# Later due times for some loads in a list scheduler, and two heads' running sums copied by engines instead of DMAs

## The chip, the core and the metric

The kernel runs on one core of a Trainium2 chip. The metric is the device time of one execution in microseconds (us). A core has five engines with queues of their own: TensorE (PE, with its weight loads shown apart as PEld), VectorE (DVE), ScalarE (ACT), GpSimd (POOL) and SyncE (SP), which here only issues DMAs. ACT can issue DMAs too. Work on different engines is ordered by semaphores alone.

## The reference

The kernel computes causal attention with a learned decay, and a two-layer network on its output:

```python
B, H, S, D = 8, 8, 576, 64
scores = q @ k.T / sqrt(D)
cum = np.cumsum(np.log(np.clip(f, 1e-4, 1.0)), axis=-1)
scores = where(causal, -1e9, scores + cum[:, :, :, None] - cum[:, :, None, :])
attn = softmax(scores); x = (attn @ v) as (B*S, H*D)
h = x @ w_in                              # 4608 x 512 @ 512 x 2048
out = (max(h, 0) + alpha * min(h, 0)) @ w_out
```

## The kernel before

The 64 heads are taken in 32 pairs `n` (four pairs to a batch). For a pair, PE makes the scores (line 332, tiles `k`, `q` or `KA`, `KB`, `QA`, `QB`), DVE takes the row maximum (L676, L594), ACT the exponentials (L552), PE transposes them (L565) and multiplies by `v`. The sums of the exponentials are inverted, written to DRAM (`rd`) and read back broadcast into the tile `ri` (L651); DVE multiplies the unnormalised output `xs` by `ri` (L744), and ACT and POOL split the product into a high and a low part (L746, L748), the `x` of the first layer. The first layer (`ffn1`) runs batch by batch, PE writing PSUM banks that ACT (L819) and DVE (L821) empty into `hs`; the second layer follows when attention is done.

The order on every engine is written by a list scheduler (`Plan`) while the program is built. Each operation has an engine, a duration in ns reckoned by a formula, a key and dependencies; the scheduler keeps a clock for each engine and repeatedly takes the operation that can start earliest (of equals, the lowest key). What it puts into an engine's queue is executed in that order on the chip, however long the waits then are. A DMA is reckoned by the issue, a shared channel of 220 KB/us and 1.0 us. An operation on the engine `"-"` issues nothing: it only takes time in the scheduler, in one queue that all of them share. The products of the first layer have the highest keys, so they fill whatever time attention leaves on PE.

The first eight pairs (`n < NN`) multiply in fp32, with two extra rows in the tiles `q` and `k` that add the decay: `cum` and plus or minus 8. For later pairs the tiles are split in two fp32r parts; their raw loads `rq` and `rk` (L488, L489) are rounded by DVE (L433), and POOL takes the remainders (L499, L504).

At the start, SP loads `f` (L345), `q` and `k` of the first pair (L443, L444). DVE clips `f` (L351), ACT takes the logarithm (L354), DVE scans (L357) in two parts, columns 0 to 255 and 256 to 575. SP and ACT then copy the sums of heads 0 and 1 by nine small DMAs (L454, L457) into the rows of `q` and `k`, as DMAs can write to any partition. POOL sets the constant rows (L373 to L375), the mask, the identity and a selection matrix. Meanwhile PE runs 21 matrix products on ones (L395) that nothing reads. SP goes on with the loads of pair 1, writes the sums of the first heads to DRAM (L362 to L364) and fetches the rows of later pairs from there (L461 to L463).

Of the kernel before, what the change touches and what calls it, by code (L numbers as in the profile page):

```python
# [8 lines left out]
F32 = mybir.dt.float32  # L9
# [9 lines left out]
NP = H // 2  # L19
# [164 lines left out]
def attention_moe(  # L184
# [79 lines left out]

    ctx_0 = ExitStack()
    p0 = ctx_0.enter_context(tc.tile_pool(name="p0", bufs=1))
    rqk = Ring(Store([(p0.tile([66, QW], F32, name=f"q0_{i}"), p0.tile([66, 2 * S], F32, name=f"k0_{i}")) for i in range(2)]))
    bch = Buf(Ring(Store([hs.rearrange("p a n -> p (a n)")[0 : B * H, 0 : 2 * S].bitcast(F32R).rearrange("p (t s) -> p t s", t=2)])))
    wbf = p0.tile([128, 512], BF16, name="wbf")
    sel = p0.tile([9, 6, 128], F32, name="sel")  # L270
# [62 lines left out]


    bft, bz, bcu = Buf(re), Buf(re), Buf(re)
    fl = lambda b: b.t[0 : B * H]
    ft, z, cu = (lambda: fl(bft)), (lambda: fl(bz)), (lambda: fl(bcu))
    chl = lambda: bch.t
    c32 = lambda: chl().bitcast(F32)
    cqf = cq.rearrange("k b t s -> (k b) t s")  # L340
# [1 line left out]

    o_w1 = op("POOL", 100, lambda: po.memset(warm, 1.0), -102)
    o_w2 = op("ACT", 1400, lambda: ac.activation(warm, warm, AF.Ln), -102, [o_w1])
    o_f = op("SP", 500, lambda: sy.dma_start(ft(), f.rearrange("b h s -> (b h) s")), -100, (), [bft], kb=144)  # L345
    o_z = op("DVE", 500, lambda: ve.memset(z(), 0.0), -100, (), [bz])

    o_clip, o_ln, o_sc = [], [], []
    PC = ((0, 256), (256, S))
    for a0, a1 in PC:  # L350
        o_clip.append(op("DVE", 130 + (a1 - a0), lambda a0=a0, a1=a1: ve.tensor_scalar(  # L351
            ft()[:, a0:a1], ft()[:, a0:a1], 1e-4, 1.0, ALU.max, ALU.min), -100, [o_f], [bft]))
    for i, (a0, a1) in enumerate(PC):
        o_ln.append(op("ACT", c_act(a1 - a0) + 180, lambda a0=a0, a1=a1: ac.activation(ft()[:, a0:a1], ft()[:, a0:a1], AF.Ln), -100, [o_clip[i]], [bft]))  # L354
    o_warm = op("ACT", 1500, lambda: ac.activation(warm, ft()[0:1, 0:1], AF.Exp), -99, o_ln, [bft])
    for i, (a0, a1) in enumerate(PC):
        o_sc.append(op("DVE", 100 + 2.2 * (a1 - a0), lambda i=i, a0=a0, a1=a1: ve.tensor_tensor_scan(  # L357
            cu()[:, a0:a1], ft()[:, a0:a1], z()[:, a0:a1], cu()[:, a0 - 1 : a0] if i else 0.0, ALU.add, ALU.add),
            -100, [o_ln[i], o_z] + o_sc, [bft, bz, bcu]))
    o_scan = o_sc[1]  # L360

# [7 lines left out]
        eng.memset(QB[64:68, S:640].bitcast(F32), 0.0)  # L369

    def eights(eng, i):
        q, k = rqk.store.items[i]
        eng.memset(q[64:66], -8.0)  # L373
        eng.memset(k[64:66], 8.0)
        eng.memset(q[64:66, S:640], 0.0)  # L375

    o_8 = [op("POOL", 2500, lambda i=i: eights(po, i), -101 + 5 * i) for i in range(2)]
    o_id = op("POOL", 600, lambda: make_identity(nc, ident), -98)

    def make_mask():  # L380

# [9 lines left out]

    o_wbf = op("DVE", 300, lambda: ve.memset(wbf, 1.0), -102)  # L392
    bw = Buf(rP)
    for i in range(7):
        op("PE", 800, lambda: [pe.matmul(bw.t, wbf[:, 0:128], wbf, start=True, stop=True) for _ in range(3)], -200, [o_wbf], [bw])  # L395

    def select():
# [7 lines left out]
            po.affine_select(sel[:, 4 + h, 64 * h : 64 * h + 64], sel[:, 4 + h, 64 * h : 64 * h + 64], pattern=[[0, 64]], base=-4,  # L405
                             channel_multiplier=1, compare_op=ALU.not_equal, fill=1.0)

    o_sel = op("POOL", 4000, select, 0.3, [o_mask])

    def zeros():  # L410
        for t in rT4.store.items:
            po.memset(t[64:128], 0.0)

    o_eps = op("POOL", 100, lambda: po.memset(eps, 1e-9), -97)
    o_zero = op("POOL", 400, zeros, -96)
    o_al = op("SP", 400, lambda: sy.dma_start(al, alpha), -4, [o_scan], kb=8)

    def signs():
# [17 lines left out]
    def early(n):  # L436
        return s_0[8 * (NN - 2)] if n == NN else None

    def load_0(n, bqk):

        b, p = divmod(n, NP)
        key = -60 if n == 0 else NS * n - 16
        ld = [op("SP", 450, lambda: sy.dma_start(bqk.t[0][0:64], qq[b, p, 0:64]), -99 if n == 0 else -59 if n == 1 else key, [o_scan] if n else (), [bqk], kb=304),  # L443
              op("SP", 450, lambda: sy.dma_start(bqk.t[1][0:64], kk[b, p, 0:64]), -99 if n == 0 else -59 if n == 1 else key, [o_scan] if n else (), [bqk], kb=288)]  # L444
        n_r = len(plan.ops)
        qr, kr = (lambda: bqk.t[0][65:66]), (lambda: bqk.t[1][64:65])
        halves = lambda ap: ap.rearrange("p (h s) -> p h s", h=2)
        rows = [[[], []] for _ in range(2)]
        if n == 0:

            for part, (a0, a1) in enumerate(PC):
                todo = [(a0, 0, a0, a1), (704 + a0, 1, a0, min(a1, S - 64))] + [(640, 1, S - 64, S)] * part
                for o, i, j0, j1 in todo:
                    rows[i][part].append(op("SP", 350, lambda o=o, i=i, j0=j0, j1=j1: sy.dma_start(  # L454
                        qr()[:, o : o + j1 - j0], cu()[i : i + 1, j0:j1]), key, [o_sc[part], o_8[n % 2]], [bcu, bqk], kb=2))
                for i in range(2):
                    rows[i][part].append(op("ACT", 600, lambda i=i, a0=a0, a1=a1: ac.dma_start(kr()[:, S * i + a0 : S * i + a1], cu()[i : i + 1, a0:a1]),  # L457
                                            -99.5, [o_sc[part], o_8[n % 2]], [bcu, bqk]))
        else:
            oo = [o_d0, o_d1, o_d2, o_8[n % 2]]  # L460
            k_ = op("SP", 350, lambda: sy.dma_start(halves(kr()), c0[0, 2 * n : 2 * n + 2].rearrange("(o h) s -> o h s", o=1)), key, oo, [bqk], kb=5)  # L461
            rows[0][0] += [k_, op("SP", 350, lambda: sy.dma_start(qr()[:, 0:S], c0[0, 2 * n : 2 * n + 1]), key, oo, [bqk], kb=2)]
            rows[1][0] += [k_, op("SP", 350, lambda: sy.dma_start(qr()[:, 640:QW], c0[1, 2 * n + 1 : 2 * n + 2]), key, oo, [bqk], kb=2)]  # L463
        c_rows.append(plan.ops[n_r:])
        return [(ld + r[0], ld + r[0] + r[1]) for r in rows]
# [17 lines left out]
    def load_n(n, bQ, bX):  # L483

        b, p = divmod(n, NP)
        kl, kc, bh = NS * n - 16, NS * n - 7, b * H + 2 * p
        bq, bk = Buf(rrq), Buf(rrk)
        l_q = op("SP", 450, lambda: sy.dma_start(bq.t, qq[b, p]), kl, [o_cl, early(n)], [bq], kb=608)  # L488
        l_k = op("SP", 450, lambda: sy.dma_start(bk.t, kk[b, p]), kl, [o_cl, early(n)], [bk], kb=576)  # L489
        QA, QB, KA, KB = ((lambda j=j: bQ.t[j]) for j in range(4))  # L490
        qc, kc_, rdy = [], [], []
        for a0, a1 in pieces(QW, 2):
            qc.append(round_(n, a1 - a0, lambda a0=a0, a1=a1: (QA()[:, a0:a1], bq.t[:, a0:a1]), kc, [l_q], [bq, bQ]))
        for a0, a1 in pieces(2 * S, 2):
            kc_.append(round_(n, a1 - a0, lambda a0=a0, a1=a1: (KA()[:, a0:a1], bk.t[:, a0:a1]), kc, [l_k], [bk, bQ]))
        qb = op("SP", 400, lambda: sy.dma_start(QB()[0:64, 0:QW].bitcast(F32), QA()[0:64].bitcast(F32)), kc, qc, [bQ], kb=304)
        rdy.append(qb)
        for i, (a0, a1) in enumerate(pieces(QW, 4)):
            rdy.append(op("POOL", c_po(a1 - a0), lambda a0=a0, a1=a1: po.tensor_tensor(  # L499
                QA()[64:128, a0:a1], bq.t[64:128, a0:a1], QA()[64:128, a0:a1].bitcast(F32), ALU.subtract),  # L500
                kc, [qc[i // 2], qb], [bq, bQ]))
        n_l = len(rdy)
        for i, (a0, a1) in enumerate(pieces(2 * S, 4)):
            rdy.append(op("POOL", c_po(a1 - a0), lambda a0=a0, a1=a1: po.tensor_tensor(  # L504
                KB()[0:64, a0:a1], bk.t[0:64, a0:a1], KA()[0:64, a0:a1].bitcast(F32), ALU.subtract),
                kc, [kc_[i // 2]], [bk, bQ]))
        rdy_x = load_x(n, bQ, bX, qc, rdy[n_l:])
        q2 = lambda: QB()[66:68].rearrange("p (h s) -> p h s", h=2)[:, :, 0:S].bitcast(F32)
        k2 = lambda: KB()[64:66].rearrange("p (h s) -> p h s", h=2).bitcast(F32)
        oo = [o_c0, o_c1, o_c2] + o_one  # L510
        rdy.append(op("SP", 350, lambda: sy.dma_start(k2(), cq[0, bh : bh + 2].rearrange("h t s -> t h s")), kc, oo, [bQ], kb=9))
        rdy.append(op("SP", 350, lambda: sy.dma_start(q2(), cqf[bh : bh + B * H + 2 : B * H + 1].rearrange("h t s -> t h s")),
                      kc, oo, [bQ], kb=9))
        return rdy, rdy_x
# [3 lines left out]
    def attention(n):  # L518
# [220 lines left out]
        def rest():  # L739
            bx, xo = Buf(rx), []  # L740
            for r in range(2):
                t0, w_ = R[r]
                st = k0 + 11.5 - hurry
                mu = op("DVE", c_dve(w_), lambda r=r, t0=t0, w_=w_: ve.tensor_tensor(bxs[r].t, bxs[r].t, bri.t[:, t0 : t0 + w_], ALU.mult),  # L744
                        st, xs_ops[r] + ri_ops, [bxs[r], bri])
                xh = op("ACT", c_acs(256), lambda r=r, t0=t0: ac.activation(  # L746
                    bx.t[:, 0, t0 : t0 + 256], bxs[r].t[:, 0:256], AF.Copy), st, [mu], [bxs[r], bx])
                xl = op("POOL", c_po(256), lambda r=r, t0=t0: po.tensor_tensor(  # L748
                    bx.t[:, 1, t0 : t0 + 256], bxs[r].t[:, 0:256], bx.t[:, 0, t0 : t0 + 256].bitcast(F32), ALU.subtract), st, [xh], [bxs[r], bx])
                xo += [xh, xl]  # L750
                x_late.extend((mu, xh, xl))
# [391 lines left out]
```

## Time and profile before

| What | us |
|---|---|
| Time, median of 3 runs | 1084.27 (1083.95 to 1085.62) |
| Time of the profiled execution | 1084.8 |
| Its span, first to last instruction | 1083.0 |
| PE busy | 1076.2 (99%) |
| DVE, ACT, POOL busy | 748.0, 683.8, 256.1 |
| Chain that ended last | PE 98%, DMA 1% |
| Mean share of the clock granted to TensorE | 0.999 |

The span is followed in us from its first instruction. A row of the timeline merges neighbouring instructions of one line. In brackets stands how long the engine had been idle before, and which instruction or DMA ended that. `SPq` and `ACTq` are DMA issues on those queues.

### The profile page before, as it was taken

Reading aid. Unit: us, or ns where it says so; the run is one execution under the profiler, and the core shown is the slowest. Engines: PE = TensorE matmul, PEld = TensorE weight load, DVE = VectorE, ACT = ScalarE, POOL = GpSimd, SP = SyncE. Lnnn points to the kernel's source line nnn. Section 1 sums busy time; section 2 is a strip of 40 time slices with the busy share of each in tenths; the row PEclk is TensorE's granted clock in tenths of the full one; section 3 lists DMA queues with packets and bytes.
Section 4 is the critical chain, followed back from the end, with each engine's and each line's share of the span. In section 5 each row is a group of like instructions: output and inputs, shape, how many; then the busy total and the mean of one; then the engine's idle time right before and its main releaser. Section 6 shows DMA issues by size and latency. Waiting matters only on the chain.

```text
span 1083.0 us, 20696 instructions
## 1 busy us (share of the span) xinstructions
PE 1076.2 (99%) x7222; PEld 933.0 (86%) x7222; DVE 748.0 (69%) x1728; ACT 683.8 (63%) x1604; POOL 256.1 (24%) x349
## 2 busy tenths in 40 slices
PE   9999999999999999999999999999999999999998
PEld 5766888878888888888887888899999999999998
DVE  6778865546555645454543885669989898989994
ACT  6878785678667867686853574556455554646551
POOL 3224774343535535434402000000000000000000
PEclk9999999999999999999999999999999999999999
DMA  6657776666867766767623765363443433443511
GB/s 153 168 162 228 223 247 189 195 196 203 238 191 223 206 210 200 228 186 222 168 83 110 247 211 196 138 210 121 140 134 117 156 118 117 139 135 122 151 61 39
DMA packets 115803, 183.57 MB, mean 170 GB/s; under 512 B 17959, under 2 KB 66878, under 8 KB 115699
## 3 DMA queue, kind: packets, MB, share of 16 engines
q1 hardware_dynamic: 115283, 181.99, 55.7%
q8 instruction: 57, 0.93, 0.4%
q14 instruction: 47, 0.39, 0.1%
q10 hardware_dynamic: 416, 0.27, 0.1%
HBM read 116.89 MB, written 49.19 MB: 153 GB/s over the span
## 4 chain that ended last, share of the span: by engine, by line
PE 98%; DMA 1%; DVE 0%; SPq 0%; issue 0%; DVEq 0%
PE bank L332 89%; PE bank L565 8%; PE bank L395 1%; DMA rq<-in_qq_dram 0%; DMA ri<-rd 0%; PE bank L698 0%; PE bank L638 0%; DVE hs L821 0%; SPq L476 0%; SPq L651 0%; SPq L477 0%; DVE xs L744 0%; DVE QA L433 0%; DVE ri L627 0%; DVE wbf L392 0%
## 5 line engine op out<-in xcount | busy, mean ns | idle before, releaser
L332 PE MATMUL bank<-xx,wi 128*128 128x512 f32 x1728 | 425.4, 396 | 0.0
L332 PEld LDWEIGHTS bank<-xx,wi 128*128 128x128 f32 x1728 | 316.4, 188 | 62.4 <-issue 0.4
L821 DVE SCALAR_TENSOR_TENSOR hs<-bank,sa,hs 128x512 f32<-128x512 f32 x96 | 71.9, 749 | 99.7 <-ACT hs L819 99.6
L332 PE MATMUL bank<-wot,xx 128*128 128x256 f32 x1008 | 123.9, 283 | 0.0
L332 PE MATMUL bank<-wi,xx 128*128 128x256 f32 x1008 | 123.9, 283 | 0.0
L332 PEld LDWEIGHTS bank<-wot,xx 128*128 128x128 f32 x1008 | 122.3, 192 | 0.0
L332 PEld LDWEIGHTS bank<-wi,xx 128*128 128x128 f32 x1008 | 122.3, 192 | 0.0
L561 ACT ACTIVATE eT<-bank 128x384 f32<-128x384 f32 x240 | 107.7, 486 | 17.5 <-PE bank L565 13.7
L552 ACT ACTIVATE e<-e,st 128x512 f32<-128x512 f32 (+2 forms) x160 | 109.5, 687 | 13.6 <-DVE st L594 8.5
L504 POOL TENSOR_TENSOR KB<-rk,KA 64x288 fp32r<-64x288 f32 x96 | 81.4, 865 | 126.6 <-DVE KA L433 81.0
L819 ACT ACTIVATE hs<-bank,ab 128x512 f32<-128x512 f32 x96 | 65.9, 687 | 60.9 <-PE bank L332 60.1
L332 PE MATMUL bank<-eT,vr 128*64 128x320 f32 (+4 forms) x896 | 90.9, 359 | 0.0
L332 PEld LDWEIGHTS bank<-eT,vr 128*64 128x64 f32 x896 | 58.4, 137 | 36.5 <-issue 3.9
L499 POOL TENSOR_TENSOR QA<-rq,QA 64x304 fp32r<-64x304 f32 x96 | 81.4, 878 | 34.6 <-DVE QA L433 32.3
L676 DVE CUSTOM_DVE_ANT_0 es<-bank,mask 128x256 f32<-128x256 f32 (+1 forms) x128 | 41.8, 354 | 65.8 <-PE bank L332 48.1
L676 DVE CUSTOM_DVE_ANT_0 e<-bank,mask 128x512 f32<-128x512 f32 (+1 forms) x128 | 75.3, 619 | 15.7 <-PE bank L332 14.3
L332 PE MATMUL bank<-KA,QA 128*128 128x288 f32 (+4 forms) x288 | 82.2, 327 | 1.7 <-DVE hs L821 1.7
L748 POOL TENSOR_TENSOR xx<-xs,xx 128x256 fp32r<-128x256 f32 x64 | 48.5, 779 | 145.7 <-ACT xx L746 145.4
L565 PEld LDWEIGHTS bank<-ident,e 128*128 128x128 f32 x576 | 69.1, 140 | 15.1 <-issue 1.9
L565 PE MATMUL bank<-ident,e 128*128 128x128 f32 x576 | 82.0, 273 | 0.0
L1037 ACT ACTIVATE xx<-gx 128x1024 fp32r<-128x1024 f32 x48 | 50.8, 1058 | 31.1 <-PE bank L332 16.1
L552 ACT ACTIVATE es<-es,st 128x256 f32<-128x256 f32 (+1 forms) x128 | 57.0, 447 | 16.3 <-DVE st L676 13.1
(142 smaller groups left out, 1649.5 us busy)
## 6 DMA issues: line engine op xcount, KB each, us to landing
hd<-hs SPq DMA_DIRECT2D x144, 256.0 KB
wx<-hd SPq DMA_DIRECT2D x47, 512.0 KB
rq<-in_qq_dram SPq DMA_DIRECT2D x24, 608.0 KB
rk<-in_kk_dram SPq DMA_DIRECT2D x24, 576.0 KB
hr<-hd SPq DMA_DIRECT2D x25, 512.0 KB
vr<-in_vv_dram SPq DMA_DIRECT2D x32, 320.0 KB
wr<-in_w_in_dram SPq DMA_DIRECT2D x16, 512.0 KB
wr<-in_w_out_dram SPq DMA_DIRECT2D x16, 512.0 KB
```

Source lines behind the costliest of these rows:

```text
L332: pe.matmul(o, lhsT, rhs, start=start, stop=stop)
L395: op("PE", 800, lambda: [pe.matmul(bw.t, wbf[:, 0:128], wbf, start=True, stop=True) for _ in range(3)], -200, [o_wbf], [bw])
L499: rdy.append(op("POOL", c_po(a1 - a0), lambda a0=a0, a1=a1: po.tensor_tensor(QA()[64:128, a0:a1], bq.t[64:128, a0:a1], QA()[64:128, a0:a1] ...
L504: rdy.append(op("POOL", c_po(a1 - a0), lambda a0=a0, a1=a1: po.tensor_tensor(KB()[0:64, a0:a1], bk.t[0:64, a0:a1], KA()[0:64, a0:a1].bitca ...
L552: ex = op("ACT", c_exp(w), lambda: ac.activation(bt.t[:, :w], bt.t[:, :w], AF.Exp, bias=lo()[:, col : col + 1], scale=-1.0, accum_out=su() ...
L561: return op("ACT", c_act(w), lambda: ac.activation(dst(), src(), AF.Copy), key, deps, [bank] + bufs)
L565: pe.transpose(t[:, c : c + 128], src[:, 128 * j : 128 * j + 128], ident)
L676: ve.tensor_tensor_reduce(out=b1.t[:, :w], in0=bS.t[:, :w], in1=mask[:, 928 - w : 928], scale=-0.125, scalar=3.0e38, op0=ALU.add, op1=ALU. ...
L748: xl = op("POOL", c_po(256), lambda r=r, t0=t0: po.tensor_tensor(bx.t[:, 1, t0 : t0 + 256], bxs[r].t[:, 0:256], bx.t[:, 0, t0 : t0 + 256]. ...
L819: cp = op("ACT", c_act(512), lambda bh=bh, bs=bs, fc=fc: ac.activation(bs.t, bh.t, AF.Relu, scale=ab[:, fc : fc + 1]), -1000, [last, o_sg] ...
L821: cp = op("DVE", c_dve(512), lambda bh=bh, bs=bs, fc=fc: ve.scalar_tensor_tensor(bs.t, bh.t, sa[:, fc : fc + 1], bs.t, ALU.mult, ALU.add), ...
L1037: his.append(op("ACT", c_acs(128 * GW * (j1 - j0)), lambda j0=j0, j1=j1, src=src, o_=o_: ac.activation(o_(0, j0, j1), src(), AF.Copy), key ...
```

## The change

Three things are done. Loads of `rq` and `rk` (pair 8 on) are followed by an operation on `"-"` of 800 ns before their users count as ready. From pair 8 on the `ri` fetches get one of 2000 ns before each of the two multiplications of a pair's halves. The sums of heads 0 and 1 are placed by engines: `f` is loaded three times, once as before and twice by ACT's queue, so that head 0 also stands in partition 64 and head 1 in partition 96; `q` and `k` of the first buffer get 97 rows, with `cum` in row 64 of `q` and row 96 of `k` (an engine writes at partitions 0, 32, 64, 96); copies by DVE (head 0, first part), ACT (head 0, second part) and POOL (head 1) replace the nine DMAs. The constants of that buffer are set by POOL and DVE; those of the second buffer, the identity and some small constants come later on POOL. Of the 21 products on ones 12 stay.

```diff
-    rqk = Ring(Store([(p0.tile([66, QW], F32, name=f"q0_{i}"), p0.tile([66, 2 * S], F32, name=f"k0_{i}")) for i in range(2)]))
+    KR = (97, 66)
+    rqk = Ring(Store([(p0.tile([KR[i], QW], F32, name=f"q0_{i}"), p0.tile([KR[i], 2 * S], F32, name=f"k0_{i}")) for i in range(2)]))
...
-    o_f = op("SP", 500, lambda: sy.dma_start(ft(), f.rearrange("b h s -> (b h) s")), -100, (), [bft], kb=144)
-    o_z = op("DVE", 500, lambda: ve.memset(z(), 0.0), -100, (), [bz])
+    f_ = f.rearrange("b h s -> (b h) s")
+    o_f = [op("SP", 500, lambda: sy.dma_start(ft()[0 : B * H], f_), -100, (), [bft], kb=144),
+           op("ACT", 600, lambda: ac.dma_start(ft()[64:96], f_[0:32]), -103, (), [bft]),
+           op("ACT", 600, lambda: ac.dma_start(ft()[96:97], f_[1:2]), -103, (), [bft])]
+    o_z = op("DVE", 500, lambda: ve.memset(z97(), 0.0), -100, (), [bz])
...
     def eights(eng, i):
-        q, k = rqk.store.items[i]
-        eng.memset(q[64:66], -8.0)
-        eng.memset(k[64:66], 8.0)
-        eng.memset(q[64:66, S:640], 0.0)
-    o_8 = [op("POOL", 2500, lambda i=i: eights(po, i), -101 + 5 * i) for i in range(2)]
-    o_id = op("POOL", 600, lambda: make_identity(nc, ident), -98)
+        if i:
+            q, k = rqk.store.items[i]
+            eng[0].memset(q[64:66], -8.0)
+            eng[1].memset(k[64:66], 8.0)
+            eng[0].memset(q[64:66, S:640], 0.0)
+            return
+        for t, r, v in zip(rqk.store.items[i], (96, 64), (-8.0, 8.0)):
+            eng[t is not rqk.store.items[i][0]].memset(t[64:97], 0.0)
+            eng[t is not rqk.store.items[i][0]].memset(t[r : r + 1], v)
+        eng[0].memset(rqk.store.items[i][0][96:97, S:640], 0.0)
+    o_8 = [op("POOL", 2500, lambda: eights((po, ve), 0), -101), op("POOL", 2500, lambda: eights((po, po), 1), -40, [o_sc[1]])]
+    op("DVE", 1200, lambda: None, -100, [o_z])
+    o_id = op("POOL", 900, lambda: make_identity(nc, ident), -98, [o_sc[0]])
...
-    for i in range(7):
+    for i in range(4):
         op("PE", 800, lambda: [pe.matmul(bw.t, wbf[:, 0:128], wbf, start=True, stop=True) for _ in range(3)], -200, [o_wbf], [bw])
...
-        qr, kr = (lambda: bqk.t[0][65:66]), (lambda: bqk.t[1][64:65])
+        qr, kr = (lambda: bqk.t[0][65:66] if n % 2 else bqk.t[0][64:65]), (lambda: bqk.t[1][64:65] if n % 2 else bqk.t[1][96:97])
...
-                todo = [(a0, 0, a0, a1), (704 + a0, 1, a0, min(a1, S - 64))] + [(640, 1, S - 64, S)] * part
-                for o, i, j0, j1 in todo:
-                    rows[i][part].append(op("SP", 350, lambda o=o, i=i, j0=j0, j1=j1: sy.dma_start(
-                        qr()[:, o : o + j1 - j0], cu()[i : i + 1, j0:j1]), key, [o_sc[part], o_8[n % 2]], [bcu, bqk], kb=2))
                 for i in range(2):
-                    rows[i][part].append(op("ACT", 600, lambda i=i, a0=a0, a1=a1: ac.dma_start(kr()[:, S * i + a0 : S * i + a1], cu()[i : i + 1, a0:a1]),
-                                            -99.5, [o_sc[part], o_8[n % 2]], [bcu, bqk]))
+                    r = 96 if i else 64
+                    todo = [(qr, (704 if i else 0) + a0, a0, S - 64 if i and part else a1)] + [(qr, 640, S - 64, S)] * (i * part) + [(kr, S * i + a0, a0, a1)]
+                    for to, o, j0, j1 in todo:
+                        e_, g_, c_ = (("DVE", ve.tensor_copy, c_dve), ("POOL", po.tensor_copy, c_po))[i] if part == 0 or i else ("ACT", lambda x, y: ac.activation(x, y, AF.Copy), c_act)
+                        rows[i][part].append(op(e_, c_(j1 - j0), lambda to=to, o=o, j0=j0, j1=j1, r=r, g_=g_: g_(
+                            to()[:, o : o + j1 - j0], c97()[r : r + 1, j0:j1]), -100.5 + 1.2 * part, [o_sc[part], o_8[0]], [bcu, bqk]))
...
+        l_q, l_k = (op("-", 800, lambda: None, kc, [l]) if n >= 2 * NP else l for l in (l_q, l_k))
...
+                late = ri_ops if n < NN else [op("-", 2000, lambda: None, st, ri_ops)]
                 mu = op("DVE", c_dve(w_), lambda r=r, t0=t0, w_=w_: ve.tensor_tensor(bxs[r].t, bxs[r].t, bri.t[:, t0 : t0 + w_], ALU.mult),
-                        st, xs_ops[r] + ri_ops, [bxs[r], bri])
+                        st, xs_ops[r] + late, [bxs[r], bri])
```

Left out of the diff: the clip and the scans run on 97 partitions in place of 64, and the later POOL constants (`eps`, the zeros of `eT`, `sel`) wait for the identity in the scheduler.

## Rows read from the trace of the kernel before

**Rows 1.** Busy time by stretch: length, engines with instruction counts, granted clock, DMA share.
```profile
0.00:8.00 8.00, 6.54 (x20) 2.50 (x21) 3.44 (x6) 3.75 (x6) 7.04 (x17) 1.00 0.41 95
...
222.00:226.00 4.00, 2.70 (x22) 2.48 (x21) 2.27 (x10) 1.81 (x5) 1.31 (x2) 1.00 0.76 246
...
555.00:1083.00 528.00, 524.33 (x3767) 495.12 (x3765) 417.40 (x749) 269.87 (x456) 7.82 (x10) 1.00 0.43 139
```

**Rows 2.** PE's waits over the whole span: total us, times, longest.
```profile
PE bank L332 <- DVE hs L821: 1.7, 2, 1.3
PE bank L395 <- DVE wbf L392: 1.5, 1, 1.5
```

**Rows 3.** Timeline of weight loads from 0 to 17 us.
```profile
6.13 0.15 PEld L395 LDWEIGHTS <-wbf 128*128 128x128 bf16 x1 [0.28 <-issue]
6.46 1.61 PEld L395 LDWEIGHTS <-wbf 128*128 128x128 bf16 x8 [0.18 <-issue]
8.19 1.29 PEld L332 LDWEIGHTS bank<-k,q 66*128 66x128 f32 x8
9.81 0.68 PEld L332 LDWEIGHTS bank<-k,q 66*64 66x64 f32 x8 [0.33 <-issue]
...
16.01 1.18 PEld L332 LDWEIGHTS bank<-k,q 66*128 66x128 f32 x8 [0.18 <-issue]
```

**Rows 4.** DMA engines' busy tenths from 0 to 16 us, 40 slices of 0.4 us.
```profile
DMA  0000078949999710000000005869899897930000
```

**Rows 5.** Timeline of SP's and ACT's DMA issues from 0 to 18 us.
```profile
0.74 0.59 SPq L345 DMA_DIRECT2D e<-in_f_dram  x1
...
5.41 1.49 ACTq L457 DMA_DIRECT2D k<-e  x2
5.42 3.11 SPq L454 DMA_DIRECT2D q<-e  x5
...
8.57 0.59 SPq L443 DMA_DIRECT2D q<-in_qq_dram  x1
...
14.71 0.21 SPq L463 DMA_DIRECT2D q<-c  x1
```

**Rows 6.** Timeline of DVE and POOL in the first 10 us.
```profile
1.47 0.54 DVE L346 MEMSET e<- 64x576 f32 x1
3.53 0.86 DVE L351 TENSOR_SCALAR e<-e 64x256 f32<-64x256 f32 x2 [1.52 <-DMA e<-in_f_dram]
4.64 0.68 DVE L357 TENSOR_TENSOR_SCAN e<-e,e 64x256 f32<-64x256 f32 x1 [0.26 <-ACT e L354]
...
5.44 0.88 DVE L357 TENSOR_TENSOR_SCAN e<-e,e,e 64x320 f32<-64x320 f32 x1
5.71 0.70 POOL masks.py:199 TENSOR_SCALAR_AFFINE_SELECT ident<-ident 128x128 f32<-128x128 f32 x1
```

**Rows 7.** Groups of one shape: busy us, mean ns of one, idle before.
```profile
L748 POOL TENSOR_TENSOR xx<-xs,xx 128x256 fp32r<-128x256 f32 x64 | 48.5, 779 | 145.7 <-ACT xx L746 145.4
L433 DVE CAST QA<-rq 128x608 fp32r<-128x608 f32 x48 | 24.5, 544 | 12.9 <-DMA rq<-in_qq_dram 12.9
```

**Rows 8.** The chain that ended last, near 220 and 400 us.
```profile
219.60 4.04 DMA ri<-rd
...
224.56 0.67 DVE hs L821
...
399.41 5.34 DMA rq<-in_qq_dram
```

**Rows 9.** Timeline of PE and DVE there.
```profile
223.73 0.83 DVE L744 TENSOR_TENSOR xs<-xs,ri 128x256 f32<-128x256 f32 x2 [5.41 <-DMA ri<-rd]
225.28 0.54 PE L332 MATMUL bank<-KA,QA 128*128 128x288 f32 x2 [1.30 <-DVE hs L821]
225.65 0.29 PE L332 MATMUL bank<-Y,X 128*128 128x288 f32 x1
225.78 0.43 PE L332 MATMUL bank<-KA,QA 128*128 128x288 f32 x2
...
406.52 0.44 PE L332 MATMUL bank<-KA,QA 128*128 128x384 f32 x1 [0.36 <-DVE hs L821]
```

**Rows 10.** Waits of DVE and SP's queue, whole span.
```profile
DVE xs L744 <- DMA ri<-rd: 21.3, 9, 5.4
DVE QA L433 <- DMA rq<-in_qq_dram: 12.9, 7, 3.3
...
SPq L651 <- DVE xs L744: 9.3, 6, 2.4
```

More of the change, by code (lines that the diff above doesn't have):

```diff
@@ L335, in attention_moe @@
     bft, bz, bcu = Buf(re), Buf(re), Buf(re)
-    fl = lambda b: b.t[0 : B * H]
-    ft, z, cu = (lambda: fl(bft)), (lambda: fl(bz)), (lambda: fl(bcu))
+    fl = lambda b: b.t[0:97]
+    ft, z97, c97 = (lambda: fl(bft)), (lambda: fl(bz)), (lambda: fl(bcu))
+    z, cu = (lambda: z97()[0 : B * H]), (lambda: c97()[0 : B * H])
     chl = lambda: bch.t
@@ L351, in attention_moe @@
         o_clip.append(op("DVE", 130 + (a1 - a0), lambda a0=a0, a1=a1: ve.tensor_scalar(
-            ft()[:, a0:a1], ft()[:, a0:a1], 1e-4, 1.0, ALU.max, ALU.min), -100, [o_f], [bft]))
+            ft()[:, a0:a1], ft()[:, a0:a1], 1e-4, 1.0, ALU.max, ALU.min), -100, o_f, [bft]))
     for i, (a0, a1) in enumerate(PC):
@@ L357, in attention_moe @@
         o_sc.append(op("DVE", 100 + 2.2 * (a1 - a0), lambda i=i, a0=a0, a1=a1: ve.tensor_tensor_scan(
-            cu()[:, a0:a1], ft()[:, a0:a1], z()[:, a0:a1], cu()[:, a0 - 1 : a0] if i else 0.0, ALU.add, ALU.add),
+            c97()[:, a0:a1], ft()[:, a0:a1], z97()[:, a0:a1], c97()[:, a0 - 1 : a0] if i else 0.0, ALU.add, ALU.add),
             -100, [o_ln[i], o_z] + o_sc, [bft, bz, bcu]))
@@ L406, in select @@
                              channel_multiplier=1, compare_op=ALU.not_equal, fill=1.0)
-    o_sel = op("POOL", 4000, select, 0.3, [o_mask])
+    o_sel = op("POOL", 4000, select, 0.3, [o_mask, o_id])
     def zeros():
@@ L412, in zeros @@
             po.memset(t[64:128], 0.0)
-    o_eps = op("POOL", 100, lambda: po.memset(eps, 1e-9), -97)
-    o_zero = op("POOL", 400, zeros, -96)
+    o_eps = op("POOL", 100, lambda: po.memset(eps, 1e-9), -97, [o_id])
+    o_zero = op("POOL", 400, zeros, -30, [o_id])
     o_al = op("SP", 400, lambda: sy.dma_start(al, alpha), -4, [o_scan], kb=8)
```

## The prediction

> **What bounds the kernel now.** I read PE's waits first, because the page has PE busy for 99% of the span. The reader is to see how short that list is [rows 2]: 1.5 us before the first product on ones, and 1.7 us in two places, both ended by DVE emptying a bank of the first layer (L821). Then the stretches [rows 1]: from 555 us to the end PE is busy for 524.33 of 528 us, and the missing 3.7 us are the last evictions and stores after its last product. So attention and first layer are packed without holes, and first-layer products fill what attention leaves. PE's own work is fixed by the operands, so its queue can get shorter in three places only: before the first scores, in the two waits, and in the products on ones. A profile with DVE at 69% and ACT at 63% has no second bound near.
>
> The start was read next [rows 3]. The weight loads of the products on ones come 0.43 us or so apart (0.15 and 0.28 idle) up to 6.13 us, and eight follow from 6.46 in 1.61 us, 0.2 each. The first scores' weights load at 8.19, with no idle time in front: nothing that PE can see was waited for, the products on ones simply ended then. The next step, the tail of the scores (64-column weights), begins at 9.81 after 0.33 us idle, and pair 1 at 16.01 after 0.18. These three moments are what the new start has to beat.
>
> **The first scores.** They need three things. (1) The products on ones: 12 in place of 21. The twelfth loads its weights at 6.13 and the thirteenth at 6.46 [rows 3], so they end near 6.5. (2) `q` and `k`: the DMA engines fall idle at 6.4 us sixteen slices of 0.4 us into the span [rows 4]. The extra 33 rows of `f` are 76 KB beside the 144 KB of the first copy and the 592 KB of `q` and `k`, moved between 2.0 and 6.4, so about 0.4 us more: 6.8, and with the notice 7.0. (3) The sums. `f` now ends with ACT's second issue: ACT's pair of issues took 1.49 [rows 5], from 0.74 to 2.2; the first copy arrived 2.2 us after its issue ended (1.33 to the clip at 3.53 [rows 5, 6]), so 4.4 at the latest. DVE has two more memsets of 1152 columns; its 576 columns took 0.54 [rows 6], so 2.16 us more, which puts the clip at 1.47 + 2.16 + 0.54 = 4.2 at the earliest. I take 4.3, 0.8 later than the 3.53 of before. The scan of part one then ends at 4.64 + 0.68 + 0.8 = 6.1. DVE's two copies of 256 for head 0 are put ahead of the second scan by their key; a cast of 608 took 0.54 [rows 7], so I take 0.27 each: 6.7. All three conditions together: about 7.0 in place of 8.19, 1.2 us earlier. The nine DMAs that go cost SP and ACT queue time, but the wait they caused was already covered by the products on ones.
>
> **Head 1 and the tail.** POOL's copies are not in this trace. The bounds per element are 0.94 ns (a memset, 0.54 us for 576 [rows 6]) and 3.0 ns (a two-operand subtraction, 779 ns for 256 [rows 7]). A copy reads one stream, so I place it nearer the memset, at 1.4: 0.36 us for 256. Part one of head 1 is then there at 6.15 + 0.72 = 6.9 (6.7 to 7.7). POOL next makes the identity, which the scheduler can start before the second scan is done: its select took 0.70 [rows 6], with the memset in front of it about 1.0. Then come the 640 elements of part two: 7.9 + 0.9 and small gaps, so 9.0, and the tail at 9.1 in place of 9.81. With the bounds: 8.6 to 10.6. The second scan ends near 6.7 + 0.88 = 7.6, and ACT's two copies of head 0 fit in before POOL's.
>
> The Trainium skill (GPSIMD Engine Reference, 4.1 Engine selection) speaks for the low bound: it says that GpSimd is about half as fast as VectorE on two-input operations and roughly at line rate with one input. No row here shows a one-input copy on POOL; by the Trainium skill's rule the copy of 256 would take about VectorE's 0.27, an estimate, the tail would come at 8.7 and the start would gain its full 0.9 (next paragraph).
>
> **Pair 1.** In the profile 6.2 us pass from the tail (9.81) to pair 1 (16.01), with PE packed; so PE is through at 9.1 + 6.2 = 15.3. The other condition is SP's queue: the five row DMAs kept it until 8.53, and the loads of pair 1 go out at 8.57 [rows 5]. They now can go out after the second scan, near 7.65, 0.9 earlier, and with them the whole row of loads to the fetch of pair 1's rows at 14.71 [rows 5], because only DMAs stand between. That would allow pair 1 at 15.1. So pair 1 starts at 15.3 in place of 16.0: **-0.7 us** (bounds -0.9, set by SP's queue, and +0.8, POOL at its upper price). From there on PE waited for nothing but the two places, so the 0.7 stay to the end. The second buffer's constants, 1216 and 1152 columns and so about 2.3 us by the memset's rate, move behind these copies to about 9 to 11.3, ahead of the fetch at 13.8, so they cost nothing; at POOL's upper price they end at 13 and the cover is gone.
>
> **The due times.** Both waits of PE have one form [rows 8, 9]. At 219.60 the third fetch of `ri` is out; it lands 4.04 us later, where the scheduler reckons about 2.4 after it. DVE has the multiplication (L744) at the head of its queue and is idle for 5.41 us; behind it stands an eviction, and PE finds no bank until that is done, 1.30 us. At 399.41 the same with `rq`, 5.34 us to land, the rounding in front of an eviction, PE idle for 0.36. With 2000 and 800 ns added, the scheduler sees the eviction ready first and puts it first. The stall goes from DVE's queue; next late is the multiplication itself, whose `x` is needed only when the first layer reaches the next batch. The pair's delays share one queue, so the last of four can be reckoned some 8 us later; as `x` fills in behind products of the batch before, that is covered. If both waits go: **-1.7 us** (bounds -1.7 and 0; above 0 is a rival). No instruction is added for this.
>
> **Sum.** -0.7 - 1.7 = -2.4 us: 1084.8 to 1082.4 for the profiled execution. That stood 0.5 above the median of 1084.27, so the median becomes **1081.9**.
>
> **The rivals.** About 0.2% (2.2 us) is what a measurement of this kernel can tell from no change; the forecast lies just beyond it.
>
> *The start gives nothing* (0.14): POOL's copies cost 3 ns per element, the tail comes at 10.6. Only the 1.7 remain: 1082.6. For it speaks that every POOL arithmetic row is that slow; against it, that a copy has one input.
>
> *The waits only move* (0.18). New due times reorder everything from pair 8 on. DVE waited 21.3 us in 9 places for `ri` and 12.9 in 7 for `rq` [rows 10], and in 14 of the 16 places PE had banks enough. Another order can uncover others of the same size: -0.7 alone, 1083.6.
>
> *Better than the forecast* (0.08): the new order also saves some of PE's small switching gaps, as the 0.33 and 0.18 of [rows 3]; five or six fewer give 1.2 more, 1080.7.
>
> *Low clock at the first scores* (0.07). The spacing of the products on ones halves only between 6.13 and 6.46 [rows 3], at the twelfth of what are now twelve, though the granted clock of that stretch reads 1.00, the 2.4 GHz level [rows 1]. If the rate rises later in another execution, the first scores run at half of it. From 1.46 to 6.3 PE ran slow, 4.9 us; as much again costs 2.4: 1084.3. Against it: after 1.30 us idle at 225.28 the clock stayed at 1.00 [rows 1], and equal pairs of products took 0.54 and 0.43 [rows 9]. The Trainium skill (TensorE: Matmul & The Clock Gate, Part 1) says that the moment of the rise is not set by a count of products and varies from run to run; by that some executions would show this rival and others not, and 12 products would be too few at times. One execution here cannot show it.
>
> *Slower* (0.08). `ri` has a single tile. A multiplication that stands later on DVE holds it longer, and the next fetch of `ri` waits in SP's queue, in order, in front of the loads of `rq` and `rk`; this took 9.3 us in 6 places already [rows 10]. If each of the 24 pairs from 8 on had such a wait grow by its 2 us, most would still be covered by first-layer products. It decides from three uncovered waits on: 3 x 2.0 - 2.4 = +3.6, 1087.9.
>
> *The forecast* has what is left, 0.45, and its own range 1081.2 to 1082.9.
>
> **How the numbers follow.** Faster by over 0.2%: 0.36 of the forecast, 0.08 of the better case, 0.03 of the first rival: 0.47. Slower: the last rival and 0.01 of the waits that move: 0.09. The rest, 0.44, is within 0.2%. The range leaves out half of the better case below and the slower rival with half of a bad reordering above: 1080.4 to 1085.0.
>
> **What would show it.** The first scores' weights at about 7.0 and with idle time in front of them; the tail near 9.1 and POOL's copies near 0.36 us for 256; pair 1 near 15.3. PE's waits for L821 gone or below 0.5 us in total, and DVE's 21.3 us for `ri` cut to a third. It is wrong if the list of PE's waits is longer than 2 us after 20 us, if the products on ones still run slow when they end, or if pair 1 starts at 16 as before.

## The result: slower by 0.31%, and the profile after

The changed kernel takes 1087.95 us (median of 10), the kernel before 1084.11 in the same series: ratio 1.0031, interval 1.0019 to 1.0042. The forecast was 1081.9, with 1085.0 as upper bound. The ten times are not one group. Beside each stands the mean clock granted to TensorE over its span:

| Executions | us | Granted clock |
|---|---|---|
| 3 | 1084.85, 1084.86, 1085.19 | 1.000 |
| 3 | 1087.91, 1087.92, 1087.98 | 0.997 |
| 4 | 1089.32, 1089.46, 1089.62, 1090.03 | 0.994 to 0.995 |

Four executions of the later series ran far longer, for a reason that these runs do not show, and stand in none of the ratios below: 1468.65 and 1173.86 us in e2 (granted clock 0.68 and 0.85), 3792.67 in e9, and 2756.87 of the kernel before in the series of e5 to e8.

The profiled execution is one of the first three: 1084.85, span 1083.1, against 1084.8 and 1083.0 before. So even with the clock kept, nothing was gained; and in seven of ten it was not kept. First PE's waits in this execution (total, times, longest), which answer to [rows 2]:

```profile
PE bank L333 <- DMA k<-in_kk_dram: 1.8, 1, 1.8
PE bank L409 <- DVE wbf L406: 1.5, 1, 1.5
PE bank L580 <- ACT es L567: 1.4, 3, 0.6
PE bank L580 <- ACT e L567: 0.2, 1, 0.2
```

The 1.7 us behind DVE's evictions (then L821, now L838) are gone. In their place stand a pause of 1.8 us before the first scores and waits of transposes (L580) for exponentials (L567), two of them in the start. The timeline of PE up to 18 us shows them; it answers to [rows 3]:

```profile
1.46 4.05 PE L409 MATMUL bank<-wbf 128*128 128x512 bf16 x12 [1.46 <-DVE wbf L406]
7.35 1.55 PE L333 MATMUL bank<-k,q 97*128 97x128 f32 x8 [1.83 <-DMA k<-in_kk_dram]
9.52 0.30 PE L580 MATMUL bank<-ident,es 128*128 128x128 f32 x1 [0.62 <-ACT es L567]
10.30 0.44 PE L580 MATMUL bank<-ident,es 128*128 128x128 f32 x2 [0.48 <-ACT es L567]
10.67 0.71 PE L333 MATMUL bank<-k,q 97*64 97x288 f32 x4
11.31 0.55 PE L580 MATMUL bank<-ident,es 128*128 128x128 f32 x3
...
16.74 1.48 PE L333 MATMUL bank<-k,q 66*128 66x128 f32 x8
```

The same rows in the kernel before:

```profile
1.46 7.10 PE L395 MATMUL bank<-wbf 128*128 128x512 bf16 x21 [1.46 <-DVE wbf L392]
8.40 3.44 PE L332 MATMUL bank<-k,q 66*128 66x128 f32 x18
...
16.04 3.51 PE L332 MATMUL bank<-k,q 66*128 66x128 f32 x18
```

The first scores start at 7.35, 1.05 earlier than the 8.40 of before. But the first half of the tail (64-column weights) comes at 10.67 in place of 9.81, because six transposes have moved in front of its halves, and pair 1 at 16.74 in place of 16.04. The other engines in that stretch answer to [rows 5, 6]:

```profile
2.66 0.60 SPq L457 DMA_DIRECT2D q<-in_qq_dram  x1
4.66 0.55 DVE L357 TENSOR_SCALAR e<-e 97x256 f32<-97x256 f32 x2
6.21 0.50 POOL L470 COPY q<-e 1x256 f32<-1x256 f32 x1
6.75 0.40 POOL L470 COPY k<-e 1x256 f32<-1x256 f32 x1
7.91 0.47 ACT L469 ACTIVATE q<-e 1x320 f32<-1x320 f32 x1 [0.69 <-POOL ident masks.py:199]
8.39 0.47 ACT L469 ACTIVATE k<-e 1x320 f32<-1x320 f32 x1
8.59 0.45 POOL L470 COPY k<-e 1x320 f32<-1x320 f32 x1
8.88 0.40 ACT L567 ACTIVATE es<-es,st 128x128 f32<-128x128 f32 x1
```

POOL's last row for the tail is written at 9.04, so the tail could have started then; PE was standing in front of a transpose. The exponential that this one needs starts at 8.88, behind ScalarE's two copies. And the loads of pair 1 go out at 2.66, not at 7.65 as I had them: no row DMA blocks SP any longer, so they run beside the load of `k` that the first scores wait for.

### The profile page after: what moved, and what is told of

Read it like the earlier page. It is cut to its first block, busy times and chain, and to the rows that moved or that the text cites. A ratio compares the mean times of both kernels' runs of the same rounds, so it can differ in the third digit from the quotient of the medians.

```text
span 1083.1 us, 20665 instructions
## 1 busy us (share of the span) xinstructions
PE 1074.4 (99%) x7213; PEld 931.1 (86%) x7213; DVE 762.5 (70%) x1732; ACT 684.5 (63%) x1606; POOL 259.8 (24%) x354
## 4 chain that ended last, share of the span: by engine, by line
PE 97%; DVE 1%; POOL 1%; ACT 1%; issue 0%; DVEq 0%; POOLq 0%
PE bank L333 89%; PE bank L580 8%; DVE xs L761 0%; PE bank L713 0%; PE bank L653 0%; ACT e L567 0%; ACT es L567 0%; POOL wi L329 0%; DVE wa L320 0%; DVE wa L323 0%; POOL q L386 0%; POOL q L387 0%; POOL mask L400 0%; DVE es L691 0%; POOL mask L396 0%
## 5 line engine op out<-in xcount | busy, mean ns | idle before, releaser
L838 DVE SCALAR_TENSOR_TENSOR hs<-bank,sa,hs 128x512 f32<-128x512 f32 x96 | 72.0, 750 | 111.1 <-ACT hs L836 110.8
L576 ACT ACTIVATE eT<-bank 128x384 f32<-128x384 f32 x240 | 109.9, 486 | 22.1 <-PE bank L580 17.8
L567 ACT ACTIVATE e<-e,st 128x512 f32<-128x512 f32 (+2 forms) x160 | 109.5, 687 | 9.0 <-DVE st L609 6.3
L580 PEld LDWEIGHTS bank<-ident,e 128*128 128x128 f32 x576 | 69.9, 140 | 16.6 <-issue 1.8
L580 PE MATMUL bank<-ident,e 128*128 128x128 f32 x576 | 83.6, 273 | 0.2 <-ACT e L567 0.2
L567 ACT ACTIVATE es<-es,st 128x256 f32<-128x256 f32 (+1 forms) x128 | 57.0, 447 | 12.1 <-DVE st L691 11.7
```

The source lines that it names most:

```text
L567: ex = op("ACT", c_exp(w), lambda: ac.activation(bt.t[:, :w], bt.t[:, :w], AF.Exp, bias=lo()[:, col : col + 1], scale=-1.0, accum_out=su() ...
L576: return op("ACT", c_act(w), lambda: ac.activation(dst(), src(), AF.Copy), key, deps, [bank] + bufs)
L580: pe.transpose(t[:, c : c + 128], src[:, 128 * j : 128 * j + 128], ident)
L838: cp = op("DVE", c_dve(512), lambda bh=bh, bs=bs, fc=fc: ve.scalar_tensor_tensor(bs.t, bh.t, sa[:, fc : fc + 1], bs.t, ALU.mult, ALU.add), ...
```

## The experiments

In the sections below *over 1087* counts executions above 1087 us, the gap between the groups of the table. Two theories: **clock** (a pause of PE in the start sends its clock back to the lower level in most executions) and, as rival, **order** (the queues' new order costs the time). Two side questions are the price of each part, and what would have to be different.

**e1: 21 products on ones in the changed kernel.**

```diff
-    for i in range(4):
+    for i in range(7):
         op("PE", 800, lambda: [pe.matmul(bw.t, wbf[:, 0:128], wbf, start=True, stop=True) for _ in range(3)], -200, [o_wbf], [bw])
```

> The changed kernel with 21 products on ones in place of 12. The mean granted clock of the ten executions of the changed kernel was 1.000, 1.000, 0.994, 0.995, 0.997, 0.997, 0.997, 0.995, 0.995 and 1.000, and its times follow it: 1084.9 to 1085.2 at 1.000, 1087.9 to 1090.0 below. Theory clock: with 12 products PE stands idle from 5.5 to 7.35 us, and in most executions the clock goes back to its lower level for some microseconds. Then 21 products, which last until the scores can start, bring the granted clock to 0.999 or more in every execution and the times to 1084.5 to 1086.2 with a spread under 2 us. Rival order: the new order of the queues makes the loss and the clock only reflects it; then the median stays at 1087 to 1089 with the same spread.

Measured: 1085.17 (1084.62 to 1085.75, 11 executions, none over 1087), ratio 1.0008 (0.9999 to 1.0017). Against the kernel before in its own series (1083.87) that is 1.3 us more, where the changed kernel stood 3.8 above (1084.11): the spread has gone and with it 2.5 us of the 3.8. The scores started at 7.81, pair 1 at 16.74 as with 12: what bounds it is not the first scores.

**e2: the kernel before with the due times alone.**

```diff
+        l_q, l_k = (op("-", 800, lambda: None, kc, [l]) if n >= 2 * NP else l for l in (l_q, l_k))
...
+                late = ri_ops if n < NN else [op("-", 2000, lambda: None, st, ri_ops)]
-                        st, xs_ops[r] + ri_ops, [bxs[r], bri])
+                        st, xs_ops[r] + late, [bxs[r], bri])
```

> The kernel before with the two due times alone (800 and 2000 ns). Theory clock: no loss of clock, and the two waits of PE for L821 (1.7 us together) go, some new ones of 0.5 us come as in the changed kernel at 149.9 and 157.0: 0.4 to 1.7 us faster than before, 1082.5 to 1083.7. Rival order: the due times cost; 1086 to 1088.

Measured: 1084.16, ratio 0.9999 (0.9991 to 1.0008). The waits for L821 are gone as expected, but no time with them. Two rows of its timeline show waits that were not there before:

```profile
149.90 0.44 PE L566 MATMUL bank<-ident,es 128*128 128x128 f32 x2 [0.34 <-ACT es L553]
156.82 0.66 PE L566 MATMUL bank<-ident,e 128*128 128x128 f32 x4 [0.15 <-ACT e L553]
```

The changed kernel has the same two (0.34 at 150.53, 0.15 at 157.41). They are 0.5 of the 1.7; the rest is taken up under e8.

**e3: the kernel before with 12 products.** The edit is that of e1 the other way, and nothing else of the change is in it.

> The kernel before with 12 products on ones in place of 21 and nothing else. Theory clock: PE is idle from the end of the products (5.5 to 6.5) until the sums arrive by DMA at about 7.4 to 8.0; granted clock below 0.998 and some 3 us more in part of the executions, the others at 1083.5 to 1084.5, since the tail's rows arrive at 9.7 in any case. Rival order: no change, 1083.2 to 1084.8 in all.

Measured: median 1096.06, 9 of 12 over 1087, up to 1098.17; the three others at 1083.05 to 1084.44. Fewer products alone cost more here than in the changed kernel. Its profile holds a lost clock. The first row is PE's timeline, the others are busy time by stretch (length, engines, granted clock, DMA share, GB/s):

```profile
7.62 6.56 PE L332 MATMUL bank<-k,q 66*128 66x128 f32 x18 [1.75 <-POOL q L373]
```

```profile
4.00:8.00 4.00, 2.25 (x9) 0.89 (x7) 1.95 (x4) 2.26 (x4) 3.67 (x9) 1.00 0.38 78
8.00:12.00 4.00, 3.96 (x15) 2.27 (x14) 1.75 (x9) 2.19 (x8) 3.61 (x15) 0.53 0.54 135
12.00:16.00 4.00, 4.00 (x14) 2.46 (x11) 1.27 (x6) 1.86 (x5) 0.00 (x0) 0.50 0.46 122
16.00:20.00 4.00, 4.00 (x10) 2.04 (x9) 1.23 (x4) 1.28 (x4) 0.00 (x0) 0.50 0.00 0
20.00:24.00 4.00, 4.00 (x21) 2.81 (x21) 3.86 (x18) 1.99 (x6) 0.00 (x0) 0.76 0.44 110
```

The scores begin at 7.62 after a pause of 1.75; soon after 8 us the granted clock is at its 1.2 GHz level (0.50), for over 12 us, although PE is busy all the time. The 18 products that took 3.44 us before take 6.56. The unchanged kernel before shows the loss too, rarely and smaller: in the same series 4 of its 35 executions have a granted clock of 0.998, and they took 1085.57 to 1086.91.

**e4: the copies by engines alone, 21 products, no due times.** The edit takes the lines of e2 out of the changed kernel and has the products of e1.

> The changed kernel without the due times and with 21 products on ones: the sums placed by engines alone. Theory clock: clock 0.999 or more in all; the first scores at 8.4, and because six transposes now stand in PE's queue in front of the tail and wait for exponentials, pair 1 starts at 16.7 to 17.7 in place of 16.0: 0.6 to 1.7 us slower than before, 1084.7 to 1085.8. Rival: the engine copies gain as forecast, 0.7 faster, 1083.4.

Measured: 1084.86, ratio 1.0008 (0.9999 to 1.0016), none over 1087. Its profile is of the slowest of the eleven (1086.80): the products on ones took 7.52 us (7.10 in the profile of before), the scores start at 8.82 and pair 1 at 17.56. So the engine copies alone, in the order that the scheduler gives them, do not speed up the start. The waits behind DVE's evictions are there again, 2.0 us.

**e5: a pause with all 21 products.** To tell the pause from the count, the kernel before sends out pair 1's loads behind pair 0's; the small copies of the sums then queue behind 592 KB.

```diff
-        ld = [op("SP", 450, lambda: sy.dma_start(bqk.t[0][0:64], qq[b, p, 0:64]), -99 if n == 0 else -59 if n == 1 else key, [o_scan] if n else (), [bqk], kb=304),
-              op("SP", 450, lambda: sy.dma_start(bqk.t[1][0:64], kk[b, p, 0:64]), -99 if n == 0 else -59 if n == 1 else key, [o_scan] if n else (), [bqk], kb=288)]
+        ld = [op("SP", 450, lambda: sy.dma_start(bqk.t[0][0:64], qq[b, p, 0:64]), -99 if n < 2 else key, [o_scan] if n > 1 else (), [bqk], kb=304),
+              op("SP", 450, lambda: sy.dma_start(bqk.t[1][0:64], kk[b, p, 0:64]), -99 if n < 2 else key, [o_scan] if n > 1 else (), [bqk], kb=288)]
```

> The kernel before, 21 products on ones, with the loads of pair 1's q and k sent out right behind those of pair 0, so that the small copies of the sums queue behind 592 KB more and the first scores wait for them until about 9.5 to 10.5 us, while the products end at 7.3 to 8.8: a pause of 1 to 3 us with all the products. Theory pause (the clock falls because PE stands idle between the products and the scores): in part of the executions the clock goes down again after the first scores and the time is 1087 to 1098, as with 12 products; the others at 1084 to 1086. Theory count (12 products are too few, whatever follows): all executions at 1084 to 1086.5.

Measured: median 1098.34, 7 of 12 over 1087 (up to 1101.90), the others at 1085.26 to 1086.70. With 21 products the clock is lost as with 12, once PE stands idle behind them: the theory *count* falls. In the profile the pause is the first row's 2.25 us; the stretches below show a clock at the lower level from about 12 to past 36 us with PE busy throughout:

```profile
10.34 5.20 PE L332 MATMUL bank<-k,q 66*128 66x128 f32 x18 [2.25 <-DMA q<-e]
```

```profile
12.00:16.00 4.00, 4.00 (x14) 2.22 (x15) 1.87 (x9) 2.03 (x8) 0.00 (x0) 0.53 0.55 123
16.00:24.00 8.00, 8.00 (x23) 5.08 (x22) 3.87 (x15) 2.93 (x8) 0.00 (x0) 0.50 0.14 38
24.00:36.00 12.00, 12.00 (x32) 6.45 (x31) 6.26 (x25) 5.42 (x18) 0.00 (x0) 0.50 0.45 110
36.00:40.00 4.00, 4.00 (x20) 1.97 (x20) 0.70 (x2) 1.78 (x7) 0.00 (x0) 0.56 0.55 131
```

**e6: POOL's copies at their measured price, 21 products.** Of the changed line only the part that differs is shown; the 21 products are the edit of e1.

```diff
-("POOL", po.tensor_copy, c_po)
+("POOL", po.tensor_copy, lambda n: 60 + 1.4 * n)
```

> The changed kernel with 21 products on ones and POOL's copies reckoned at 60 + 1.4 n ns, near what they took, in place of 60 + 2.3 n; this alone puts both halves of the tail in front of the six transposes in PE's queue. Theory: the loss at the start is PE waiting for the exponentials behind which the tail stands. Then the tail starts at 9.1 to 9.3, pair 1 near 15.5 in place of 16.74, and the time is 1.2 us under the 1085.17 with the old order: 1083.9 to 1084.2. Rival (the order does not matter, ScalarE's copies in front of the exponentials do): pair 1 at 16.5 or later, 1085.

Measured: 1083.96, ratio 0.9996 (0.9987 to 1.0004), 1.2 us under e1, as expected (1.3 by the two ratios, each against the kernel before in its own series). In PE's timeline the tail now follows the scores without a pause (16 products in one row), the transposes come behind it:

```profile
8.55 2.60 PE L333 MATMUL bank<-k,q 97*128 97x128 f32 x16
11.08 0.87 PE L580 MATMUL bank<-ident,es 128*128 128x128 f32 x6
...
16.00 3.44 PE L333 MATMUL bank<-k,q 66*128 66x128 f32 x18
```

Pair 1 starts at 16.00, not at 15.5: the products on ones took 7.25 us in this execution and held the scores until 8.55.

**e7 and e8: one more look at each kernel, unchanged.**

> The changed kernel once more, for a trace of an execution in which the clock is lost, which 7 of 10 were. Theory clock: if the time is over 1087, the granted clock of the first 24 us lies well under 1.00, PE's products in it take twice as long, and nothing after it differs from the first trace by more than 0.5 us in all. Rival order: the difference lies in waits of PE elsewhere.

Measured: 1089.96. PE's timeline and the stretches of this execution of the changed kernel:

```profile
7.30 1.55 PE L333 MATMUL bank<-k,q 97*128 97x128 f32 x8 [0.54 <-POOL k L470]
9.60 0.30 PE L580 MATMUL bank<-ident,es 128*128 128x128 f32 x1 [0.75 <-ACT es L567]
10.39 0.66 PE L580 MATMUL bank<-ident,es 128*128 128x128 f32 x2 [0.48 <-ACT es L567]
```

```profile
8.00:12.00 4.00, 2.76 (x11) 1.09 (x10) 1.29 (x8) 3.28 (x11) 3.74 (x10) 0.81 0.56 128
12.00:16.00 4.00, 4.00 (x12) 1.98 (x11) 1.18 (x5) 1.36 (x3) 2.48 (x11) 0.50 0.01 2
16.00:20.00 4.00, 4.00 (x6) 1.58 (x5) 3.04 (x12) 1.42 (x4) 0.00 (x0) 0.50 0.00 0
20.00:24.00 4.00, 4.00 (x28) 2.92 (x26) 2.88 (x14) 2.44 (x7) 0.00 (x0) 0.91 0.60 133
24.00:60.00 36.00, 36.00 (x250) 24.92 (x248) 26.48 (x92) 30.48 (x100) 7.92 (x11) 1.00 0.65 180
```

Three pauses, then about 10 us at the lower level, and 1.00 from 24 us on. The span is 5.1 us longer than in the first trace (1088.2 to 1083.1): about 10 us at half the clock are 5 us of work. No wait elsewhere is new.

> The kernel before once more. Its profiled execution stood 0.9 us above the median of its 35 runs, 1083.87. If its two waits for L821 (1.7 us) vary with the time that the loads take to land, this trace shows them at another size, 0.3 to 1.0 us in all, and a shorter span; if the waits are fixed by the order, it shows 1.6 to 1.8 again.

Measured: 1084.76, span 1083.0. PE's waits in the second trace of the kernel before:

```profile
PE bank L332 <- DVE hs L821: 0.9, 1, 0.9
PE bank L332 <- DMA q<-c: 0.8, 1, 0.8
```

One wait for L821 in place of two. It is half of what the first trace had, though the order is the same. The span did not shrink, as was expected, because pair 1 waited 0.8 us for its row by DMA and started at 16.79 in place of 16.04.

From the start of pair 1 to the end of the span, all at a granted clock of 1.00 from there on, four traces without the due times took 1065.6 (e3), 1066.2 (e8), 1067.0 (the first trace of before) and 1067.4 us (e4), with 0.2, 0.9, 1.7 and 2.0 us of waits behind DVE's evictions. So such a wait costs what it lasts, but its mean in these four is 1.2, not 1.7. Seven traces with the due times (the changed kernel, e1, e2, e6, e7, e9, e10) took 1066.0 to 1066.5 with no such wait, 0.6 to 1.2 us more than the 1065.3 to 1065.4 that the other four would leave without theirs. The due times take away the spread; on the mean they gain about 0.3 us.

**e9 and e10: fewer products with the price of e6,** 18 and 12 (`range(6)` and `range(4)`).

> The changed kernel with POOL's copies reckoned at 60 + 1.4 n ns and 18 products on ones. Their end moves with the moment at which the clock rises, which the traces so far show between 4.1 and 7.2 us: 6.6 to 8.2 us, while the scores' data are there at 7.35. Theory pause: pauses of PE up to 0.7 us in front of the scores and 0.3 in front of the tail; if pauses of that size keep the clock, all executions lie at 1083.2 to 1084.2 and the median 0.1 to 0.4 under the 1083.96 with 21; if they do not, some are above 1087. Theory count (18 are enough or not by themselves) gives the same first case, so this run measures the margin and does not tell the two apart.

> The same with 12 products. The pause in front of the scores stays (0.5 to 1.8 us), those behind the first scores (0.78 and 0.68 us) become one of some 0.3. If the pause in front of the scores is enough to lose the clock, most executions are at 1086 to 1090 as with the changed kernel; if the pauses behind it are what loses it, nearly all are at 1083 to 1084.5.

Measured: 18 products 1083.39, ratio 0.9992 (0.9983 to 1.0001); 12 products 1083.46, ratio 0.9995 (0.9986 to 1.0004), 10 of 11 below 1083.8 and one at 1086.26 (granted clock 0.996). The median with 18 is 0.6 under e6, where 0.1 to 0.4 was expected. In their profiles pair 1 starts at 15.28 and 15.29, as the forecast had it (15.3). With 12 products one pause remains in the start:

```profile
PE bank L333 <- POOL k L470: 0.8, 1, 0.8
```

So the pause before the scores seldom loses the clock when the two behind the scores are gone; with 12 products and those two, 7 of 10 lost it; with two behind the scores, of 0.24 and 0.48 us, and none before them (e1), none of 11. A single pause is enough where it is longer: e3 and e5 have one each in the start, of 1.75 and 2.25 us in their traces, and lost the clock in 9 and 7 of 12. But length alone does not decide. The first trace of the changed kernel kept its clock through 1.83, 0.62 and 0.48 us, and e7 lost it after 0.54, 0.75 and 0.48. What else it takes stays open. The version with 18 products is the quickest measured, 0.08% under the kernel before, which this measurement can hardly tell from no change.

## Why the prediction was wrong

**The products on ones** are the step that failed first. I costed nine fewer at nothing but a gain, and kept the clock as a rival at 0.07 and 2.4 us. The evidence against it was a pause of 1.30 us at 225 us, in the middle of dense work, after which the clock stayed [rows 1, 9]; I carried that over to the start. There PE pauses three times (1.83, 0.62, 0.48 in the first trace, which kept the clock; 0.54, 0.75, 0.48 in e7, which lost it) and the loss is the rule: 7 of 10, 3.1 to 5.2 us each over the 1084.85. e1 prices it at 2.5 of the median, e3 and e5 show it without the rest of the change. I also put the end of 12 products at 6.5 from one trace; the weight loads of ones halve their spacing at a moment of their own in each execution, and 12 products took 4.05 us in one and 5.30 in another, 21 took 6.35 to 7.52.

The Trainium skill (TensorE: Matmul & The Clock Gate, Part 1) said as much: the moment of the rise varies from run to run and no count of products sets it. Here the traces agree (4.05 and 5.30 us for the same 12). But what cost the time was not a late rise.

**The start, -0.7, came out at +0.7** (pair 1 at 16.74 against 16.04; the second trace of before has 16.79, but e1 and e4 stand 1.3 and 1.0 above before in their medians). Its prices held: POOL's copy of 256 took 0.40 to 0.50 (0.36 forecast, bounds 0.24 to 0.78), the last row for the tail was there at 9.04 (9.0 forecast), the scores started at 7.35 (7.0). What failed is *6.2 us pass from the tail to pair 1 with PE packed*: I moved a stretch of PE's queue as if its order stayed. The scheduler reckons POOL's copy of 256 at 649 ns (60 + 2.3 x 256), believes the rows late and puts transposes in front of the tail, which wait for exponentials that ScalarE's copies delay. e6 changes only that price and gets 1.2 us back. With that price and fewer products (e9, e10) pair 1 does start at 15.3. And SP's queue was misread: pair 1's loads went out at 2.66, before the scan that I had them wait for, so SP was no bound. They run beside the load of `k`, which came last in the first trace; how much they delayed it no run shows, and it is little, because in e7 and e10 the scores start at 7.30 and 7.21 behind POOL's copy. One reading was also of the wrong engine: the lower bound of 0.94 ns for POOL is from a memset of VectorE [rows 6]. POOL's own took 1.10 us for 1216 elements, 0.90 ns each, so nothing hangs on it.

**The due times, -1.7,** did to the order what I said: L821 is gone from PE's waits, DVE's for `ri` fell from 21.3 to 3.0 us. But the time is nearer the rival *the waits only move*: e2 gives 0.9999. The 1.7 was the size of one execution: the four traces without the due times have 0.2 to 2.0, 1.2 in the mean. And 0.6 to 1.2 us came in elsewhere, 0.5 of it in new waits for exponentials. Where the rest of that lies stays open; it is below what the medians resolve. The three steps together (2.5, 1.4, and 1.4 to 1.7) make 5.3 to 5.6 of the 6.2 us between the forecast's -2.4 and the measured +3.8.

**Rivals.** The *slower* one was the wrong mechanism. SP's waits in front of the `ri` fetches did grow (9.3 us in 6 places to 12.9 in 5), but the list of PE's waits has none for a load behind them. *Low clock* named the right quantity, at 2.4 us and a chance of 0.07, where it came in 7 of 10 at 3.1 to 5.2 us each; it makes most of the 3.8. Its mechanism was another, though: a rate that rises too late. In e7 the first eight scores took 1.55 us, as in the trace with the clock kept, so the clock had risen; it fell behind them, after the pauses.

## What to carry to other kernels

Work that nobody reads can be holding up the clock; before it is cut, look at where PE pauses in the microseconds after it, and take many executions, with the granted clock of each: one trace can keep the clock where most lose it. When a list scheduler writes the order, a part that becomes faster than it is reckoned does not move up by itself: give it its measured price, or something else stands in front of it. A wait that hangs on when a transfer lands has another length in each execution, so one trace does not give what it is worth.

## What the runs showed of the hardware

Once lost, the clock stayed at its lower level for 10 to 27 us although PE was busy in every one of those stretches (e7: 12 to 20 us at 0.50 with 4.00 of 4.00 busy; e5: 16 to 36 us). What PE did there were fp32 scores and transposes. In e7 and e3 it rose again amid that work, near 20.6 and 21.8 us; in e5 at 39.5, when the products with `v` had begun at 37.07. So this work does not keep the clock down for good; why it takes so long the runs do not tell. The granted clock also reads 1.00 in the first stretch, while the products on ones still run at half their later rate, so a clock of 1.00 at the very start says nothing there.

One-row copies cost POOL 0.45 us for 320 elements against 0.47 on ScalarE, and VectorE 0.28 to 0.40 for 256 against POOL's 0.40 to 0.50.
